# A fused SiLU layer on one core: the first weight slab loaded in two halves, three loads issued from ScalarE, and the first transposed blocks copied by VectorE alone

## Chip, cores and metric

The kernel runs on one core of a Trainium2 chip. The metric is the device time of one execution in microseconds (us), given as the median of several runs of the same program. TensorE is the matrix engine, VectorE and ScalarE the two engines that here copy and evaluate results, GpSimd a fourth one that only prepares constants, and SyncE an engine whose queue issues DMA transfers. ScalarE has a queue that can issue them too. PSUM is the memory that TensorE writes its results to, in eight banks. SBUF is the memory that holds operands.

## What is computed

`x` has 2048 rows of 640, `w1` is 640 x 1728 and `w2` is 1728 x 640, all bf16.

```python
def reference(x, w1, w2):
    h = jnp.einsum("bsd,df->bsf", x, w1)
    h = silu(h)
    out = jnp.einsum("bsf,fd->bsd", h, w2)
    return out
```

## The kernel before

TensorE sums over the partition axis of both its operands, so the first product needs x with its 640 features on partitions. The features are cut into five slabs of 128 (`DT = 5`), the 1728 hidden columns into 13 tiles of 128 (`FT`) and a tail of 64 (`FL`), and the 2048 rows into four chunks of 512 (`SCH`). The result `hT` of the first product keeps the hidden columns on partitions, as the second product needs them.

**Chunks one to three** are brought into `xT` by transposing DMAs (line 153). **Chunk zero** can't wait for those: its four blocks of 128 rows are loaded as they lie, into `x0` (lines 125, 126, 131), and TensorE transposes them, five times 128 x 128 for a block, by a product with an identity matrix. This is the helper `turn` (line 170). The transposed block lies in PSUM and is copied to `xT`: the first three of its five parts by VectorE (line 180) from one bank, the other two by ScalarE (line 188) from a second bank.

**The first weights.** Of w1, the first six tiles of hidden columns (`FA = 6`, 768 columns) are loaded apart from the rest, in five slabs, one for each 128 features (line 129, `ld_k`), 192 KB each. The other columns follow in two larger loads (line 134). All of these transfers, and the loads of x, are issued by SyncE through the helper `load` (line 89), each with a semaphore of its own, in the order x block 0, x block 1, slab 0, slab 1, x block 2, slab 2, x block 3, slab 3, slab 4, the two larger loads. They are issued ahead of a barrier that all engines meet at the start: `barrier_wait_here(ET.SP)` (line 137) moves SyncE's wait for that barrier behind them. ScalarE's wait for it stays at the head of its program. Behind it ScalarE evaluates SiLU once on a small tile (line 147), which brings the function's table in early.

**TensorE's order for chunk zero** is written out by hand in lines 196 to 244. Nine products on a zeroed tile `z` (line 168, `dummies`) run before anything has landed; they write to PSUM bank 3 and nothing reads them. Then the first two blocks are turned, and two more dummies run. The six tiles are accumulated in six PSUM banks at once, slab by slab, by the helper `k_pass(k, j0, j1)` (line 212): for each of the six tiles, one product of slab `k` with the columns of blocks `j0` to `j1`, over the partitions of slab `k`. The hand-written order, with what each step waits for:

```python
wait(pe, *t0, ld_k[0])
k_pass(0, 0, 1, first=True)
wait(pe, *t1)
k_pass(0, 1, 2)
wait(pe, ld_k[1])
k_pass(1, 0, 2)
t2 = turn(2, 7, 6)
wait(pe, ld_k[2])
k_pass(2, 0, 2)
wait(pe, *t2)
```

Then slabs 0 to 2 are used on block 2 alone, block 3 is turned, slab 3 is used on three blocks, slabs 0 to 3 on block 3 alone, and slab 4 on all four. TensorE runs its program in order, so a wait holds everything behind it. In the profile `turn`'s products have line 177, those of every pass have line 204 (the helper `mm`), and the SiLU evaluations have line 208. The seven remaining hidden tiles of chunk zero, the other chunks and the second product follow, and are not touched by the change.

Of the kernel before, what the change touches and what calls it, by code (L numbers as in the profile page):

```python
# [9 lines left out]
def bass_standalone__dense_activation_silu__prompt_kernel(  # L10
# [13 lines left out]
    P = 128  # L24
    NB = 8
    BANK = 512
    DT = D // P
# [10 lines left out]
    pe, act, dve, pool, sp = nc.tensor, nc.scalar, nc.vector, nc.gpsimd, nc.sync  # L38

    with ExitStack() as es:  # L40
        def sb(name, shape, dtype):
            return es.enter_context(nc.sbuf_tensor(name, shape, dtype))
# [3 lines left out]
        w1s = sb("w1s", [P, DT, F], bf16)  # L46
# [14 lines left out]
        def sem(name):  # L61
            s = es.enter_context(nc.semaphore(name))
            count[s.name if hasattr(s, "name") else name] = 0
            return [s, 0]

        def tick(ins, s, n=1):
            ins.then_inc(s[0], n)
            s[1] += n
            return (s, s[1])

        def wait(eng, *points):
            for pt in points:
                if pt is None:
                    continue
                s, v = pt
                key = (id(eng), id(s))
                if seen.get(key, 0) < v:
                    eng.wait_ge(s[0], v)
                    seen[key] = v
# [6 lines left out]
        def load(eng, out_ap, in_ap):  # L86
            s = sem(f"s_ld{n_dma[0]}")
            n_dma[0] += 1
            return tick(eng.dma_start(out=out_ap, in_=in_ap), s, 16)  # L89
# [21 lines left out]
        def barrier_wait_here(engine):  # L111
            lst = nc.main_func.blocks[0].instructions
            lst.append(lst.pop(preamble(engine, "EventSemaphore")))

        x_v = xf.rearrange("(j p) d -> p j d", p=P)
        w1_v = w1.rearrange("(dt p) f -> p dt f", p=P)
        w2_v = w2[0:F0, :].rearrange("(ft p) d -> p ft d", p=P)

        FA = 6
# [4 lines left out]
        p_z = ahead_of_start(lambda: tick(dve.memset(z[:, :], 0.0), s_dve), ET.DVE)  # L124
        ld_x[0] = load(sp, x0[:, 0, :], x_v[:, 0, :])
        ld_x[1] = load(sp, x0[:, 1, :], x_v[:, 1, :])
        ld_k = []
        for k in range(DT):
            ld_k.append(load(sp, w1s[:, k, 0:FA * P], w1_v[:, k, 0:FA * P]))
            if k in (1, 2):  # L130
                ld_x[k + 1] = load(sp, x0[:, k + 1, :], x_v[:, k + 1, :])
        for a, b in FG:
# [33 lines left out]
        def dummies(n):  # L166
            for _ in range(n):
                pe.matmul(ps[:, 3, 0:HB], lhsT=z[:, 0:P], rhs=z[:, :], start=True, stop=True)  # L168

        def turn(j, b_v, b_a):  # L170
            wait(pe, ld_x[j], p_ident, bank_free[b_v], bank_free[b_a])
            v = ps[:, b_v, :].bitcast(bf16)
            a = ps[:, b_a, :].bitcast(bf16)
            nv = DT if b_a == b_v else 3
            for dt in range(DT):
                dst = v[:, dt * P:(dt + 1) * P] if dt < nv else a[:, (dt - nv) * P:(dt - nv + 1) * P]
                ins = pe.transpose(dst, x0[:, j, dt * P:(dt + 1) * P], ident[:, :])  # L177
            t = tick(ins, s_pe)
            wait(dve, t)
            r = tick(dve.tensor_copy(  # L180
                out=xT[:, 0:nv, j * P:(j + 1) * P],
                in_=v[:, 0:nv * P].rearrange("p (k s) -> p k s", s=P),
            ), s_dve)
            bank_free[b_v] = r
            pts = [r]
            if nv < DT:
                wait(act, t)
                r = tick(act.copy(  # L188
                    out=xT[:, nv:DT, j * P:(j + 1) * P],
                    in_=a[:, 0:(DT - nv) * P].rearrange("p (k s) -> p k s", s=P),  # L190
                ), s_act)
                bank_free[b_a] = r
                pts.append(r)
            return pts

        wait(pe, p_z)
        dummies(9)
        barrier_wait_here(ET.PE)
        t0 = turn(0, 7, 6)
        t1 = turn(1, 5, 4)  # L200
        dummies(2)

        def mm(o, l, r, start, stop, shared=False):
            return pe.matmul(o, lhsT=l, rhs=r, start=start, stop=stop, skip_group_check=shared)  # L204

        def silu(out_ap, in_ap, bank, after):
            wait(act, after)
            r = tick(act.activation(out=out_ap, in_=in_ap, func=ACT.Silu), s_act)  # L208
            bank_free[bank] = r
            return r  # L210

        def k_pass(k, j0, j1, first=False, last=False):
            for ft in range(FA):
                if first:
                    wait(pe, bank_free[ft])
                ins = mm(
                    ps[:, ft, j0 * P:j1 * P],
                    w1s[:, k, ft * P:(ft + 1) * P],
                    xT[:, k, j0 * P:j1 * P],
                    start=first, stop=(k == DT - 1), shared=True,  # L220
                )
                if last:
                    silu(hT[:, ft, 0:SCH], ps[:, ft, :], ft, tick(ins, s_pe))

        wait(pe, *t0, ld_k[0])
        k_pass(0, 0, 1, first=True)
        wait(pe, *t1)
        k_pass(0, 1, 2)
        wait(pe, ld_k[1])
        k_pass(1, 0, 2)  # L230
        t2 = turn(2, 7, 6)
        wait(pe, ld_k[2])
        k_pass(2, 0, 2)
# [178 lines left out]
```

## Time and profile before

| | |
|---|---|
| median of 5 runs | 126.49 us (126.29 to 126.83) |
| the profiled execution | 126.29 us |
| its span, first to last instruction | 124.8 us |
| TensorE busy | 122.0 us, 98% of the span |
| ScalarE busy | 39.9 us, 32% |
| VectorE busy | 9.0 us, 7% |
| nine dummies on TensorE | from 0.39 us, 2.10 us |
| first two turns on TensorE | from 2.34 us, 1.25 us |
| two dummies | from 3.38 us, 0.63 us |
| ScalarE's table load (line 147) | from 0.73 us, 1.28 us; its activation from 2.02 us, 0.23 us |
| VectorE's first two copies (line 180) | from 3.10 and 3.63 us, 358 ns each |
| ScalarE's first two copies (line 188) | from 3.09 and 3.63 us, 372 ns each |
| VectorE's wide casts (line 287) | 692 ns for 512 columns, 557 ns for 384, from fp32 |
| one product of 128 columns, of 256 | 219 ns, 272 ns from start to result |
| third and fourth turn, first product | 5.85 and 7.85 us (weights from 5.75 and 7.80 us) |
| first pass of slab 2 | weights from 6.08 us, products from 6.13 us |

Times inside the execution count from the start of its span. A duration is that of one instruction from its start to its result; products are pipelined, so that a row of them takes less than the sum of its durations. The chain of waits goes back from the last instruction: at each step to what released it, or to the instruction before it on its engine. In a window's row the columns are the stretch, its length, the busy time and number of instructions of TensorE, of its weight loads, of VectorE, ScalarE and GpSimd, then the granted clock, the mean busy share of the 16 DMA engines, and the GB/s that they moved. In the row of a DMA issue stand what was moved, the issuing queue (SPq is SyncE's, ACTq ScalarE's), how many, the KB of each, and the median us from issue to landing; a KB here is 1024 bytes.

### The profile page before, as it was taken

The page shows a single profiled execution, that of the slowest core. Times are in us where ns is not written, and L with a number is a line of the kernel's source. Part 1 is how long each engine was busy: PE and PEld are TensorE (multiplying, and loading weights), DVE is VectorE, ACT ScalarE, POOL GpSimd, SP SyncE. Part 2 cuts the span into 40 slices and gives each one's busy share as a digit, 9 for nine tenths or more (in the row PEclk, how much of TensorE's full clock was granted, in tenths as well). Part 3 has the DMA queues.
Part 4 walks back from the last instruction along what each step waited for, and adds up shares of the span by engine and source line. Part 5 has one row for each costly group of instructions (what it writes and reads, how often), then busy time and mean ns, then how long its engine had stood idle before and what let it go on. Part 6 is the DMA issues. An engine that isn't in the chain of part 4 may idle for free.

```text
span 124.8 us, 1496 instructions
## 1 busy us (share of the span) xinstructions
PE 122.0 (98%) x653; PEld 58.4 (47%) x653; DVE 9.0 (7%) x16; ACT 39.9 (32%) x70; POOL 0.8 (1%) x7
## 2 busy tenths in 40 slices
PE   8899999999999999999999999999999999999993
PEld 6686444444444444444444443444444443444452
DVE  0220000000000000000000004202020210112021
ACT  4225955555555555555530003010101001010100
POOL 2000000000000000000000000000000000000000
DMA  6989953446970000000000001341111111111112
GB/s 173 277 265 250 137 115 86 108 102 132 374 271 5 0 0 3 0 0 5 0 0 0 0 0 42 85 147 57 54 53 53 53 53 53 53 58 53 53 59 99
DMA packets 17255, 10.37 MB, mean 83 GB/s; under 512 B 10849, under 2 KB 17249, under 8 KB 17249
## 3 DMA queue, kind: packets, MB, share of 16 engines
q1 hardware_dynamic: 17104, 10.21, 31.2%
q8 instruction: 5, 0.08, 0.3%
q10 hardware_dynamic: 144, 0.07, 0.2%
q14 instruction: 2, 0.01, 0.0%
HBM read 5.16 MB, written 2.62 MB: 62 GB/s over the span
## 4 chain that ended last, share of the span: by engine, by line
PE 95%; DMA 3%; SPq 1%; issue 0%; ACT 0%
PE ps L204 94%; DMA w1s<-in_w_dram 3%; SPq L89 1%; PE ps L177 0%; ACT o_sb L289 0%; SPq L397 0%
## 5 line engine op out<-in xcount | busy, mean ns | idle before, releaser
L204 PE MATMUL ps<-xT,w1s 128*128 128x512 bf16 (+4 forms) x328 | 59.1, 348 | 0.5 <-DMA w1s<-in_w_dram 0.5
L204 PE MATMUL ps<-w2s,hT 128*128 128x512 bf16 (+2 forms) x221 | 45.4, 367 | 0.0
L204 PEld LDWEIGHTS ps<-xT,w1s 128*128 128x128 bf16 (+1 forms) x328 | 28.8, 98 | 30.4 <-DVE xT L180 1.0
L208 ACT ACTIVATE hT<-ps 128x512 bf16<-128x512 f32 x52 | 30.3, 602 | 23.2 <-PE ps L204 23.2
L204 PEld LDWEIGHTS ps<-w2s,hT 128*128 128x128 bf16 x221 | 20.9, 98 | 24.4 <-issue 1.1
L289 ACT CAST o_sb<-ps 128x512 bf16<-128x512 f32 (+1 forms) x8 | 4.4, 545 | 42.2 <-PE ps L204 42.2
L204 PE MATMUL ps<-hT,w2s 128*128 128x512 bf16 x52 | 11.4, 379 | 0.0
L287 DVE CAST o_sb<-ps 128x512 bf16<-128x512 f32 (+1 forms) x9 | 6.1, 677 | 39.9 <-PE ps L204 39.9
L204 PEld LDWEIGHTS ps<-hT,w2s 128*128 128x128 bf16 x52 | 5.0, 97 | 6.3 <-issue 0.4
L287 DVE CAST oT<-ps 128x512 bf16<-128x512 f32 x2 | 1.3, 686 | 66.8 <-PE ps L204 66.8
L289 ACT CAST oT<-ps 128x512 bf16<-128x512 f32 x2 | 1.1, 588 | 11.1 <-PE ps L204 11.1
L168 PE MATMUL ps<-z 128*128 128x256 bf16 x11 | 2.7, 419 | 0.4 <-DVE z L124 0.4
L188 ACT COPY xT<-ps 128x256 bf16<-128x256 bf16 x4 | 1.5, 372 | 5.0 <-PE ps L177 5.0
L204 PE MATMUL ps<-w2t,hTt 64*128 64x512 bf16 (+2 forms) x17 | 2.2, 366 | 0.0
L177 PE MATMUL ps<-ident,x 128*128 128x128 bf16 x20 | 2.1, 265 | 0.0
L180 DVE COPY xT<-ps 128x384 bf16<-128x384 bf16 x4 | 1.4, 358 | 6.9 <-PE ps L177 6.9
L168 PEld LDWEIGHTS ps<-z 128*128 128x128 bf16 x11 | 1.5, 144 | 0.8 <-DVE z L124 0.4
L177 PEld LDWEIGHTS ps<-ident,x 128*128 128x128 bf16 x20 | 1.6, 118 | 0.4 <-DMA x<-in_x_dram 0.3
L208 ACT ACTIVATE hTt<-ps 128x512 bf16<-128x512 f32 x2 | 1.2, 597 | 1.1 <-PE ps L204 1.1
L147 ACT ACT_TABLE_LOAD x1 | 1.3, 1283 | 0.7 <-PEq L397 0.7
L204 PEld LDWEIGHTS ps<-w2t,hTt 64*128 64x128 bf16 x17 | 0.7, 94 | 1.4 <-issue 0.8
L204 PE MATMUL ps<-hTt,w2t 64*128 64x512 bf16 x4 | 0.6, 381 | 0.0
(10 smaller groups left out, 1.5 us busy)
## 6 DMA issues: line engine op xcount, KB each, us to landing
out_dram<-o_sb SPq DMA_DIRECT2D x15, 160.0 KB, 1.8
w2s<-in_w_dram SPq DMA_DIRECT2D x1, 1120.0 KB, 6.6
w1s<-in_w_dram SPq DMA_DIRECT2D x5, 192.0 KB, 3.6
w2s<-in_w_dram SPq DMA_DIRECT2D x1, 960.0 KB, 9.3
x<-in_x_dram SPq DMA_DIRECT2D x4, 160.0 KB, 2.9
w1s<-in_w_dram SPq DMA_DIRECT2D x1, 640.0 KB, 6.7
w1s<-in_w_dram SPq DMA_DIRECT2D x1, 560.0 KB, 7.9
xT<-in_x_dram SPq DMA_TRANSPOSE x15, 2.8
```

Source lines behind the costliest of these rows:

```text
L89: return tick(eng.dma_start(out=out_ap, in_=in_ap), s, 16)
L147: act.activation(out=warm[:, :], in_=warm[:, :], func=ACT.Silu)
L168: pe.matmul(ps[:, 3, 0:HB], lhsT=z[:, 0:P], rhs=z[:, :], start=True, stop=True)
L177: ins = pe.transpose(dst, x0[:, j, dt * P:(dt + 1) * P], ident[:, :])
L180: r = tick(dve.tensor_copy(out=xT[:, 0:nv, j * P:(j + 1) * P], in_=v[:, 0:nv * P].rearrange("p (k s) -> p k s", s=P),), s_dve)
L188: r = tick(act.copy(out=xT[:, nv:DT, j * P:(j + 1) * P], in_=a[:, 0:(DT - nv) * P].rearrange("p (k s) -> p k s", s=P),), s_act)
L204: return pe.matmul(o, lhsT=l, rhs=r, start=start, stop=stop, skip_group_check=shared)
L208: r = tick(act.activation(out=out_ap, in_=in_ap, func=ACT.Silu), s_act)
L287: r = tick(dve.tensor_copy(out=out_ap, in_=in_ap), s_dve)
L289: r = tick(act.copy(out=out_ap, in_=in_ap), s_act)
```

## The change

Slab 0 is loaded in two halves of three tiles each, with a semaphore for each half. The first half is issued by ScalarE, as are slabs 1 and 3; all three stand in ScalarE's program behind its barrier wait and ahead of its SiLU on the small tile. The second half of slab 0, slabs 2 and 4, the blocks of x and the larger loads stay with SyncE, in their order. `turn` takes a new argument: for blocks 0 and 1, VectorE copies all five parts from one bank, and ScalarE none; blocks 2 and 3 are as before. One dummy follows the second turn instead of two. `k_pass` can be limited to some of the six tiles, and slab 0 is used on its first three tiles for block 0, then for block 1, then on the other three for block 0 and block 1, with the wait for the second half between.

```diff
+        FH = 3
+        ld_k0a = load(act, w1s[:, 0, 0:FH * P], w1_v[:, 0, 0:FH * P])
         ld_k = []
         for k in range(DT):
-            ld_k.append(load(sp, w1s[:, k, 0:FA * P], w1_v[:, k, 0:FA * P]))
+            lo = FH if k == 0 else 0
+            q = act if k in (1, 3) else sp
+            ld_k.append(load(q, w1s[:, k, lo * P:FA * P], w1_v[:, k, lo * P:FA * P]))
...
-        def turn(j, b_v, b_a):
+        def turn(j, b_v, b_a, split=True):
...
-            nv = DT if b_a == b_v else 3
+            nv = 3 if split else DT
...
-        t0 = turn(0, 7, 6)
-        t1 = turn(1, 5, 4)
-        dummies(2)
+        t0 = turn(0, 7, 6, False)
+        t1 = turn(1, 5, 4, False)
+        dummies(1)
...
-        def k_pass(k, j0, j1, first=False, last=False):
-            for ft in range(FA):
+        def k_pass(k, j0, j1, first=False, last=False, fts=range(FA)):
+            for ft in fts:
...
-        wait(pe, *t0, ld_k[0])
-        k_pass(0, 0, 1, first=True)
+        wait(pe, *t0, ld_k0a)
+        k_pass(0, 0, 1, first=True, fts=range(FH))
         wait(pe, *t1)
-        k_pass(0, 1, 2)
+        k_pass(0, 1, 2, fts=range(FH))
+        wait(pe, ld_k[0])
+        k_pass(0, 0, 1, first=True, fts=range(FH, FA))
+        k_pass(0, 1, 2, fts=range(FH, FA))
```

## The prediction

> **What bounds the kernel now.** I read the chain of waits first, in order of time (start us, length us, what):
>
> ```profile
> 0.99 3.41 DMA w1s<-in_w_dram
> 4.40 0.14 issue
> 4.53 1.49 PE ps L204 x18
> 6.02 0.28 PE ps L177 x5
> 6.30 1.72 PE ps L204 x24
> 8.02 0.28 PE ps L177 x5
> 8.29 114.60 PE ps L204 x579
> ```
>
> After the first w1 slab lands at 4.40, TensorE never waits again until 122.89. So the change can move the end only by what it does to TensorE's waits in the first 10 us, and one microsecond lost there is lost at the end. Call the slabs k0 to k4 and the blocks of x x0 to x3. The timeline of SyncE's queue gives the times of issue, one every 0.475 us (the nine small loads, then the two large w1 loads):
>
> ```profile
> 0.09 0.86 SPq L89 DMA_DIRECT2D x<-in_x_dram  x2
> 0.99 0.91 SPq L89 DMA_DIRECT2D w1s<-in_w_dram  x2
> 1.94 0.43 SPq L89 DMA_DIRECT2D x<-in_x_dram  x1
> 2.41 0.43 SPq L89 DMA_DIRECT2D w1s<-in_w_dram  x1
> 2.89 0.43 SPq L89 DMA_DIRECT2D x<-in_x_dram  x1
> 3.36 1.95 SPq L89 DMA_DIRECT2D w1s<-in_w_dram  x4
> ```
>
> The issues asked for one at a time from the third on, k0, k1, x2, k2, x3, k3, k4 (last figure: us from issue to landing):
>
> ```profile
> w1s<-in_w_dram SPq DMA_DIRECT2D x1, 192.0 KB, 3.4
> w1s<-in_w_dram SPq DMA_DIRECT2D x1, 192.0 KB, 3.4
> x<-in_x_dram SPq DMA_DIRECT2D x1, 160.0 KB, 3.5
> w1s<-in_w_dram SPq DMA_DIRECT2D x1, 192.0 KB, 3.6
> x<-in_x_dram SPq DMA_DIRECT2D x1, 160.0 KB, 3.8
> w1s<-in_w_dram SPq DMA_DIRECT2D x1, 192.0 KB, 4.1
> w1s<-in_w_dram SPq DMA_DIRECT2D x1, 192.0 KB, 4.9
> ```
>
> Issue plus landing time gives k0 4.40, k1 4.87, x2 5.44, k2 6.01, x3 6.69, k3 7.46, k4 8.73. The delay grows along the queue, from 3.4 to 4.9 us: issuing is not what holds the loads, moving the bytes is. The windows say the same (last two columns: busy share of the DMA engines, GB/s):
>
> ```profile
> 2.00:3.00 1.00, 1.00 (x10) 0.63 (x9) 0.00 (x0) 0.24 (x2) 0.00 (x0) 1.00 0.90 283
> 3.00:4.00 1.00, 1.00 (x8) 0.54 (x6) 0.72 (x2) 0.74 (x2) 0.00 (x0) 1.00 0.96 272
> 4.00:5.00 1.00, 0.49 (x10) 0.50 (x10) 0.00 (x0) 0.00 (x0) 0.00 (x0) 1.00 0.96 261
> 5.00:6.00 1.00, 1.00 (x16) 0.93 (x14) 0.00 (x0) 0.00 (x0) 0.00 (x0) 1.00 0.97 295
> ```
>
> The engines are 90 to 97% busy at a mean of 278 GB/s. The second thing to see is hidden in the chain: between the landing of k0 and the first matmul lie 0.13 us (4.40, 4.53). With the same 0.13, k2, landed at 6.01, allows its pass at 6.14, and that pass does start at about 6.13, when the second turn has ended. k2 is thus on time by nothing. Two limits meet there, and removing the first wait alone exposes the second.
>
> **The change part by part.**
>
> *Order of the loads.* ScalarE's first action behind the barrier is at 0.73 (its table load in the timeline). Three issues at 0.475 us put k0's first half at 0.73, k1 at 1.20, k3 at 1.68. SyncE, with k1 and k3 gone and k0 halved, issues x0 0.09, x1 0.53, k0's second half 0.99, x2 1.47, k2 1.94, x3 2.42, k4 2.89. Merged by time of issue and summed in KB: x0 160, x1 320, first half 416, second half 512, k1 704, x2 864, k3 1056, k2 1248, x3 1408, k4 1600. Before, k2 stood at 1056, x3 at 1216, k3 at 1408. All other places are as they were: k3 has gone ahead of k2 and x3, though it is needed only after both.
>
> *Price of that.* 192 KB are 196.6 thousand bytes, and at 278 GB/s 0.71 us: k2 lands at 6.01 + 0.71 = 6.72. A second price by the landings: place 1248 lies 32/192 of the way from the old place 1216 (6.69) to 1408 (7.46), so 6.82, or 0.81 later. No row shows two queues loading together, so I bound it: 0 if k3's bytes stay behind k2's, 0.81 if all are ahead, and below nothing if two queues together move more than 278 GB/s (the windows from 9 to 11 us show 339 and 355). I take 0.71, since k3 is issued 0.26 us ahead of k2 and the engines have no idle share to carry it in.
>
> The Trainium skill speaks against the change here (DMA: Bandwidth & Descriptors, "Issuing engines are not separate DMA queues"): transfers issued by ScalarE and SyncE run on the same 16 DMA engines and interleave, and a second issuer saves issue time alone. No run shown here has two load queues. By that rule the rate stays and the sum is the one taken; without it the sum would be that of the rival with the higher rate below.
>
> *The split of k0.* The first half stands at 416, halfway from x1's 320 (asked the same way, it landed 2.3 after its issue at 0.53: 2.83) to k0's 512 (4.40): 3.62. Six of the twelve matmuls of 128 columns can then run before 4.53. Their pace is 18 matmuls in 1.49 us, made of 24 column-blocks of 128 and a last result's 0.16 (272 ns less two blocks), so 0.056 each, and six save 0.33. The second half lands where k0 did, 4.40: six matmuls from 4.53 end at 4.87 instead of 5.20. Next late is k1: 4.87 + 0.13 = 5.00 starts its pass, 12 blocks or 0.67 take it to 5.67, the second turn of five transposes (0.28) to 5.95. Then k2 is waited for, and even at its old landing this is until 6.14. So the 0.33 is worth nothing at the end. Shorter rows cost nothing I can see: the large w1 loads, with rows of 1024 and 896 bytes instead of 1536, ran at the 339 and 355 GB/s.
>
> *VectorE alone.* Five blocks instead of three per copy. 384 columns take 358 ns. The fp32 casts of 512 and 384 columns (692, 557 ns) give 1.05 ns a column and 152 ns fixed; with that fixed part bf16 costs 0.54 a column, so 640 columns 496 ns; at 1.05 it would be 627. I take 0.50: the copies run 3.10 to 3.60 and 3.63 to 4.13 (4.38 at the dear end), both under the second half's 4.53. Uncovered, the second would hold six matmuls to 4.2. ScalarE's two copies of 372 ns go.
>
> *Table load and silu's first use* move behind three issues: 0.73 + 1.43 = 2.16, and 1.28 + 0.23 later 3.67. The next work queued there is the third turn's copy, at 6.33 before: covered by 2.7 us.
>
> *One dummy less* takes 0.21 us (2.10 less one result's 0.42, over 8) out of TensorE's wait: nothing on the path, but see the clock.
>
> *SyncE's later issues*, the two large loads and the transposing loads, come 0.95 us earlier but stand behind the same bytes. The first large load lands at 4.31 + 6.7 = 11.0; the first SiLU starts at 10.86, five tiles of 0.22 before the pass ends and that load is needed, some 11.9; the delay adds slack.
>
> *Behind k2*: pass at 6.72 + 0.13 = 6.85 instead of 6.13. x3 lands at k3's old 7.46, needed at 7.80 + 0.72; k3 is early; k4 at 8.73 is needed past 10. Nothing more is lost or won back. **Sum: +0.72 us.** The profiled execution took 126.29 around its span of 124.8, and is the fastest of the five; on it the sum gives 127.01, on the median of 126.49 it gives 127.21. I name the middle, 127.1.
>
> **Rivals.**
>
> *Higher rate, faster.* Two queues fill what one leaves, and the loads run at the 345 GB/s of 9 to 11 us. The bytes through k2, now 1248 KB or 1278 thousand, take 3.70 us from about 1.1, so 4.8, and with x1's lag (328 thousand bytes moved by 2.4, with 222 GB/s from 1 to 2 us and 283 after, landed 2.83) k2 lands near 5.3. Then TensorE is held by the second copy: 4.13 + 0.05, three matmuls (0.17), six (0.33), the k1 pass (0.67), the turn (0.28): k2's pass at 5.63, 0.50 early: 125.99. It decides from about 300 GB/s on, where k2 lands below 6.01. Against it: the engines are already 90% busy and more with one queue. Chance 0.21.
>
> *k3 doesn't get ahead, no change.* If ScalarE's third load starts 0.3 us later than I reckon, or its queue gets the smaller turn, k2 keeps 6.01 and its pass 6.13: 126.49, with 0.3 either way. For it: the margin at issue is only 0.26. Chance 0.17.
>
> *ScalarE late or a cold clock, much slower.* Were the table load issued first, ScalarE's loads would start at 2.01, 2.49, 2.96; k1 would stand behind x3, at 1216 KB, land at 6.69, and its pass start at 6.82 instead of 5.20: 128.1. Against it: the profile gives the table load the line of the activation it serves, L147, which the code has behind the new loads. The clock: nine dummies run at 0.21 per 256 columns, where the passes from 4.53 run at 0.11. The pace doubled between 3.8 and 4.53, after an unbroken busy TensorE since 0.39. If waits and the missing dummy delay that past k2's pass, its 30 blocks (12, then 18) cost 0.05 more each: 1.5, or 128.7. Chance of both 0.10.
>
> The Trainium skill puts that change of pace at some 3.4 us of sustained work (TensorE: Matmul & The Clock Gate, Part 1); by it, the 3.4 us are filled before the first new wait, and the clock costs nothing.
>
> **How the numbers follow.** A measurement of this kernel tells from no change what exceeds 0.3%, 0.38 us: slower is above 126.87, faster below 126.11. The forecast has 0.52, with its own range 126.9 to 127.4 (from the prices 0.71 and 0.81, on 126.29 or 126.49). Slower 0.52 + 0.10 = 0.62, same 0.17, faster 0.21. The range reaches to the faster rival and past the dearer price, 125.9 to 127.6, and leaves out the much slower one.
>
> **What would show it.** Right: in the changed kernel's chain of waits a DMA of w1s ends near 6.7 and TensorE waits some 0.5 to 0.9 us ahead of the third slab's pass; the first matmuls start near 4.2; the rate from 2 to 6 us stays below 300 GB/s; k3 lands before k2. Wrong: TensorE unbroken from about 4.2 on, a rate near 340, k2 landing by 6.0, or ScalarE's issues behind the table load.

## The result and the profile after

The changed kernel takes a median of 126.97 us over 43 runs, the kernel before 126.58 us over 80 runs beside it. The ratio is 1.0028, with a 95% interval from 1.0017 to 1.0038: slower by 0.35 us. The ratio leaves out the few executions that lie more than 1.5% above the fastest of their kernel, so it differs a little from that of the two medians. The forecast's sum was 0.72 us. The direction held and the size came out at half of that sum.

The profiled execution took 126.41 us, the fastest of its 43, so it shows the change at its best. Its chain of waits in order of time (start us, length us, what; the passes now have line 208, the turns line 181 and the dummies line 172, and the lines shift by one or two with other edits):

```profile
0.53 2.95 DMA x<-in_x_dram
3.48 0.05 issue
3.52 0.73 PE ps L181 x5
4.25 0.02 issue
4.28 0.50 DVE xT L184
4.78 0.05 issue
4.83 1.33 PE ps L208 x15
6.16 0.28 PE ps L181 x5
6.43 1.72 PE ps L208 x24
...
8.43 114.60 PE ps L208 x579
```

The wait that sets the end is no longer the first slab's. Block 1 of x lands at 3.48 instead of 2.80. Its turn and VectorE's copy follow, and TensorE runs without a wait from 4.83 on. Slab 2's pass begins at 6.27 instead of 6.13, so this execution loses 0.14 us there.

The timelines of ScalarE and VectorE in the same execution show the moved work:

```profile
0.73 1.34 ACTq L89 DMA_DIRECT2D w1s<-in_w_dram  x3
2.11 1.28 ACT L151 ACT_TABLE_LOAD   x1 [2.11 <-issue]
...
4.28 0.49 DVE L184 COPY xT<-ps 128x640 bf16<-128x640 bf16 x1 [0.71 <-PE ps L181]
```

Three issues from the barrier on, the table load behind them, a copy of five parts in 0.49 us: these stand as the forecast had them. The windows (the last two columns are again the DMA engines' busy share and the GB/s) don't:

```profile
2.00:3.00 1.00, 1.00 (x8) 0.48 (x6) 0.00 (x0) 0.89 (x1) 0.00 (x0) 1.00 0.94 254
3.00:4.00 1.00, 0.51 (x6) 0.48 (x6) 0.49 (x1) 0.62 (x2) 0.00 (x0) 1.00 1.01 329
4.00:5.00 1.00, 0.73 (x10) 0.52 (x8) 0.49 (x1) 0.00 (x0) 0.00 (x0) 1.00 1.02 343
5.00:6.00 1.00, 1.00 (x16) 0.93 (x14) 0.00 (x0) 0.00 (x0) 0.00 (x0) 1.00 1.03 365
```

From 3 to 6 us the loads run at 329 to 365 GB/s, where one queue gave 261 to 295. The forecast kept 278.

Landings, from the trace's semaphore events, in us from the span's start:

| | forecast | this execution | a second one (a_same, below) |
|---|---|---|---|
| block 1 of x | 2.83 | 3.48 | 3.12 |
| slab 0, first half | 3.62 | 3.69 | 3.35 |
| slab 0, second half | 4.40 | 4.37 | 4.91 |
| slab 1 | 4.87 | 4.64 | 5.12 |
| block 2 of x | 5.44 | 5.41 | 5.86 |
| slab 3 | 6.01 (slab 2's old place) | 5.59 | 6.27 |
| slab 2 | 6.72 | 6.01 | 6.45 |

In both, slab 3 lands ahead of slab 2, as forecast. In the first, slab 2 still lands when it did before (5.97 by the same events, where the forecast has 6.01 from a rounded time).

### The profile page after: what moved, and what is told of

Read it like the earlier page. It is cut to its first block, busy times and chain, and to the rows that moved or that the text cites. A ratio compares the mean times of both kernels' runs of the same rounds, so it can differ in the third digit from the quotient of the medians.

```text
span 124.9 us, 1493 instructions
## 1 busy us (share of the span) xinstructions
PE 121.9 (98%) x652; PEld 58.3 (47%) x652; DVE 9.2 (7%) x16; ACT 39.2 (31%) x68; POOL 0.8 (1%) x7
## 4 chain that ended last, share of the span: by engine, by line
PE 95%; DMA 2%; DVE 0%; SPq 0%; issue 0%; ACT 0%
PE ps L208 94%; DMA x<-in_x_dram 2%; PE ps L181 1%; DVE xT L184 0%; SPq L89 0%; ACT o_sb L296 0%; SPq L404 0%
## 5 line engine op out<-in xcount | busy, mean ns | idle before, releaser
L184 DVE COPY xT<-ps 128x640 bf16<-128x640 bf16 (+1 forms) x4 | 1.7, 425 | 6.8 <-PE ps L181 6.8
L192 ACT COPY xT<-ps 128x256 bf16<-128x256 bf16 x2 | 0.7, 372 | 4.5 <-PE ps L181 4.5
```

What stands on the lines that cost most here:

```text
L184: r = tick(dve.tensor_copy(out=xT[:, 0:nv, j * P:(j + 1) * P], in_=v[:, 0:nv * P].rearrange("p (k s) -> p k s", s=P),), s_dve)
L192: r = tick(act.copy(out=xT[:, nv:DT, j * P:(j + 1) * P], in_=a[:, 0:(DT - nv) * P].rearrange("p (k s) -> p k s", s=P),), s_act)
```

## The experiments

Three theories. **K**, the forecast's: slab 3 goes ahead of slab 2, which then lands late. **X**, formed from the profile above: block 1 of x shares the DMA engines with slab 0's first half, lands late, and VectorE's copy holds TensorE. **C**: TensorE is idle for longer, and the pace of its products doubles later. The expectations call this its clock; the granted clock stands at 1.00 in every window, so only the pace of the products shows it. Each kernel was timed in five rounds beside the kernel before; the four of a group ran on one chip.

### First group: undo one part

**a_same** is the changed kernel again.

> The changed kernel once more, for a second profile and a time on the same chip as the next three. Theory K (the forecast's: slab 3 gets ahead of slab 2, which then lands late): ratio to the kernel before 1.003, and slab 2 lands after 6.4 us with TensorE waiting for it. Theory X (the rival formed from the changed kernel's profile: slab 0's first half shares the DMA engines with block 1 of x, which lands some 0.6 us later, and VectorE's longer copy of 0.49 us then holds TensorE): ratio 1.003, block 1 lands after 3.2 us, TensorE starts behind that copy after 4.6 us, and no wait for slab 2.

Measured: 1.0047 (1.0022 to 1.0073). Its chain ends otherwise than that of the first profile:

```profile
1.94 4.51 DMA w1s<-in_w_dram
6.45 0.05 issue
6.49 1.83 PE ps L208 x24
8.33 0.28 PE ps L181 x5
8.61 114.60 PE ps L208 x579
```

Here slab 2, issued at 1.94, lands at 6.45, and its pass starts at 6.49 instead of 6.13: 0.36 us lost, just the median's loss. Block 1 was late as well (3.12), but what it delayed came back in the wait for slab 2. Two executions of one program end on two different waits; one profile could have led to either theory.

**a_k3_sp** gives slab 3 back to SyncE:

```diff
-            q = act if k in (1, 3) else sp
+            q = act if k == 1 else sp
```

> The changed kernel with slab 3 back on SyncE, behind block 3 of x. Theory K: slab 2 gets its old place, the loss of 0.35 us is gone, ratio 1.000. Theory X: block 1 of x still shares with slab 0's first half, so ratio 1.003 as before the edit.

Measured: 1.0012 (0.9994 to 1.0029), 0.35% below a_same on the same chip. K expected 1.000, X 1.003: the interval holds the first and ends just short of the second. Against the 1.0028 of the 43 runs the gain is only 0.16%. Its profile fell on an execution of 127.2 us, which shows something else:

```profile
0.99 4.13 DMA w1s<-in_w_dram
5.12 0.05 issue
5.17 1.77 PE ps L208 x12
6.95 0.28 PE ps L181 x5
7.22 1.72 PE ps L208 x24
```

Slab 1's pass and the rest of slab 0's are 18 column-blocks of 128 and should take about 1.2 us at the pace of the kernel before (18 times 0.056, and 0.16 for the last result); they take 1.77. TensorE's fast pace began only near 6.5 us here. This is taken up again below.

**a_split** copies the first two blocks on both engines again:

```diff
-        t0 = turn(0, 7, 6, False)
-        t1 = turn(1, 5, 4, False)
+        t0 = turn(0, 7, 6)
+        t1 = turn(1, 5, 4)
```

> The changed kernel with the first two blocks copied by VectorE and ScalarE together again. Theory X: the second copy ends 0.13 us earlier, so 0.12 us of the loss come back, ratio 1.002. Theory K: the copies are under the loads, ratio stays 1.003.

Measured: 1.0018 (0.9995 to 1.0041). The interval holds both expectations, so this run is inconclusive. In its profile ScalarE's copy (0.38 us) stands where VectorE's stood, and TensorE starts at 4.85, no sooner than in the changed kernel.

**a_all_sp** puts every load on one queue, the split of slab 0 kept:

```diff
-        ld_k0a = load(act, w1s[:, 0, 0:FH * P], w1_v[:, 0, 0:FH * P])
+        ld_k0a = load(sp, w1s[:, 0, 0:FH * P], w1_v[:, 0, 0:FH * P])
...
-            q = act if k in (1, 3) else sp
+            q = sp
```

> The changed kernel with all loads on SyncE's queue, slab 0 still in two halves, behind block 1 of x. Both theories lose their cause: K because slab 3 is behind slab 2, X because block 1 is ahead of slab 0. Ratio 1.000 by both; block 1 lands at 2.8 us as before. A ratio still near 1.003 would put the cause into the split, the single dummy or VectorE's copies.

Measured: 1.0012 (0.9988 to 1.0036), median 126.99. Block 1 lands at 2.83 again. In the profiled execution (127.47, the slowest of its twelve) TensorE waits 1.2 us for slab 2, issued at 2.89 and landed at 7.30; 15 of its 16 parts had landed by 6.54. The split alone brings nothing. Whether its extra issue, which here delays every later load, costs something, the interval doesn't tell: it holds 1.003, and all twelve runs lie above the median of the kernel before beside them (126.60). So this run does not show that the loss goes with both causes.

### Second group: one part alone, and other orders

**b_k3_first** makes the change of place alone, on the kernel before and its one queue:

```diff
-        for k in range(DT):
+        for k in (0, 1, 3, 2, 4):
...
```

> The kernel before with one change of order on SyncE's queue: slab 3 is issued ahead of slab 2 and block 3 of x. One queue, so nothing shares. Theory K at the forecast's price: slab 2 lands 0.7 us later, at 6.7 us, its pass starts near 6.85, ratio 1.005 to 1.006. Theory X (the loss comes from block 1 of x sharing with slab 0's first half, and VectorE's longer copy): block 1 is untouched, ratio 1.000.

Measured: 1.0054 (1.0033 to 1.0076), which is 0.68 us. The forecast's price for a place in the line was 0.71 to 0.81. X expected nothing. The profiled execution was the slowest of six (127.58); its chain shows the kind of wait:

```profile
2.89 4.52 DMA w1s<-in_w_dram
7.41 0.05 issue
7.46 1.83 PE ps L205 x24
```

Slab 2 is issued at 2.89, one place later than before, and TensorE stands until it lands. Of its 16 parts 15 had landed by 6.79, near the forecast's 6.72; the last came 0.6 us later.

**b_act** moves whole slabs 1 and 3 to ScalarE, without any other part of the change:

```diff
-            ld_k.append(load(sp, w1s[:, k, 0:FA * P], w1_v[:, k, 0:FA * P]))
+            ld_k.append(load(act if k in (1, 3) else sp, w1s[:, k, 0:FA * P], w1_v[:, k, 0:FA * P]))
```

> The kernel before with slabs 1 and 3 issued by ScalarE behind the barrier and nothing else changed: slab 0 whole, two dummies, copies on both engines. Theory K: slab 3 is ahead of slab 2, ratio 1.003 to 1.006. Theory X: slab 1 now takes the place of slab 0's first half beside block 1 of x and delays slab 0 as well; ratio 1.002 to 1.004, with block 1 landing after 3.1 us. Theory R (two queues together move more than one, which is why the forecast's 0.72 us came out at half): 300 GB/s or more from 2 to 6 us, where one queue shows 277.

Measured: 1.0176 (1.0149 to 1.0203), far past what any theory gave, in all six runs (128.21 to 129.34). The chain:

```profile
0.53 4.16 DMA x<-in_x_dram
...
5.87 2.56 PE ps L204 x18
8.43 0.53 PE ps L177 x5
8.97 1.74 PE ps L204 x24
```

Block 1 of x, beside a whole slab on the other queue, lands at 4.69. TensorE's first 18 products then start at 5.87 instead of 4.53 and take 2.56 us instead of 1.49, the turn behind them 0.53 instead of 0.28: the slow pace lasts until near 9 us. Of the 2.7 us that this execution loses, 1.3 come from the late start and 1.3 from the slow pace. Of block 1's 16 parts 15 had landed by 3.10, so what came late is one part, and that sharing caused this is not shown. Why all six runs lie so high was not tried further. The rate from 2 to 6 us was 331 GB/s, as theory R had it.

**v1** keeps one queue, and orders loads and passes by need:

```diff
-            if k in (1, 2):
-                ld_x[k + 1] = load(sp, x0[:, k + 1, :], x_v[:, k + 1, :])
+            if k in (2, 3):
+                ld_x[k] = load(sp, x0[:, k, :], x_v[:, k, :])
...
-        t2 = turn(2, 7, 6)
         wait(pe, ld_k[2])
         k_pass(2, 0, 2)
+        t2 = turn(2, 7, 6)
+        wait(pe, ld_k[3])
+        k_pass(3, 0, 2)
         wait(pe, *t2)
-        for k in range(3):
+        for k in range(4):
             k_pass(k, 2, 3)
         t3 = turn(3, 7, 6)
-        wait(pe, ld_k[3])
-        k_pass(3, 0, 3)
+        wait(pe, ld_k[4])
+        k_pass(4, 0, 3)
         wait(pe, *t3)
         for k in range(4):
             k_pass(k, 3, 4)
-        wait(pe, ld_k[4])
-        k_pass(4, 0, 4, last=True)
+        k_pass(4, 3, 4, last=True)
```

> The kernel before, one queue, but loads and passes in another order: slab 2 ahead of block 2 of x and slab 3 ahead of block 3, and TensorE uses slab 2 on blocks 0 and 1 before it turns block 2, then slab 3, and slab 4 on three blocks before block 3. If the bytes that must have landed at each step set the start (the ground of theory K), each step has about 0.4 us more slack, and a late slab costs less: ratio 0.998 to 1.000. If the waits ahead of slab 1 decide, ratio 1.000.

Measured: 1.0016 (0.9998 to 1.0035), above what either ground expected, though the interval reaches 1.000. In its profile no wait follows slab 0's landing at 4.18:

```profile
4.32 2.54 PE ps L204 x24
```

TensorE's passes begin 0.21 us sooner than in the kernel before. But these 24 products are 36 column-blocks, which take 2.2 us at the pace of the kernel before; the fast pace began only near 5.2 us, and this took back more than the early start gave.

**v2** has this order on the changed kernel, with ScalarE issuing slab 0's first half, slab 1 and block 2 of x.

> The changed kernel with the order of v1; ScalarE issues slab 0's first half, slab 1 and block 2 of x, SyncE all else, so that no load goes ahead of one needed sooner. Theory K: its cause is gone and the second queue's rate is left, ratio 0.997 to 1.000. Theory X: block 1 of x still shares and VectorE still copies alone, ratio 1.001 to 1.003.

Measured: 1.0032 (1.0009 to 1.0054), at the upper end of X's expectation and against K's. Its chain goes through slab 0's second half, landed at 5.31, with block 1 at 3.09. With no slab out of order, the second queue still didn't pay, so K is not all that two queues can lose by.

### Third group: what was priced at nothing, and TensorE's pace

**b_small** is the kernel before with VectorE's copies and the single dummy:

```diff
-            nv = DT if b_a == b_v else 3
+            nv = DT if j < 2 else 3
...
-        dummies(2)
+        dummies(1)
```

> The kernel before with the two edits that the forecast priced at nothing: VectorE alone copies blocks 0 and 1, and one dummy instead of two follows the turns. All loads as before. Theory K (slab 3 ahead of slab 2) and the forecast: the copies end at 4.13 us, ahead of slab 0 at 4.4 us, ratio 1.000. Theory C (waits and the missing dummy leave TensorE idle, and its clock rises later in some executions): the idle time ahead of slab 0 grows by 0.2 us to 0.7 us, ratio 1.001 to 1.002. Theory X (the longer copy holds TensorE): ratio 1.001.

Measured: 0.9999 (0.9980 to 1.0018). In its profile slab 0 happened to land at 4.12, so that the copy was last:

```profile
3.69 0.50 DVE xT L180
4.20 0.05 issue
4.25 1.82 PE ps L204 x18
```

Even uncovered, the copy lets TensorE start at 4.25, earlier than the 4.53 of the kernel before. Its 18 products take 1.82 us instead of 1.49, since the fast pace began near 5.0 here. The times show no cost of the two edits, to about 0.2%.

**a_warm** fills TensorE's idle time in the changed kernel:

```diff
         t0 = turn(0, 7, 6, False)
+        dummies(1)
         t1 = turn(1, 5, 4, False)
-        dummies(1)
+        dummies(3)
```

> The changed kernel with one more dummy between the first two turns and three instead of one behind them, so that TensorE is idle for about 0.6 us less before slab 0's second half. Loads as changed. Theory C: executions with a late clock go, ratio 1.000 to 1.002 instead of 1.003 to 1.005. Theory K: ratio stays 1.003 to 1.005. Theory X: the same, as block 1 and the copy are not moved.

Measured: 1.0007 (0.9986 to 1.0028), as C expected and below the 1.003 of K and X, though its interval meets a_same's. Its profiled execution (127.34) waits for slab 2 all the same:

```profile
1.94 5.23 DMA w1s<-in_w_dram
7.18 0.05 issue
7.22 1.83 PE ps L209 x24
```

Here 15 of slab 2's 16 parts had landed by 6.57.

**a_warm_k3** adds the edit of a_k3_sp to it.

> a_warm with slab 3 back on SyncE behind block 3, as in a_k3_sp (1.0012 there). Theories K and C together: both causes gone, ratio 0.998 to 1.000. Theory X: 1.001 or more is left, since block 1 still shares with slab 0's first half and VectorE copies alone.

Measured: 0.9983 (0.9960 to 1.0005), the lowest of all, not told apart from the kernel before. Taking slab 3 back again gained, 0.24% here and 0.35% in the first group. Their mean is 0.30%; with the half-widths of the four intervals combined as independent (each difference about 0.31, their mean 0.22) it is above nothing. By the same reckoning the added dummies gain as much, 0.40% (a_same to a_warm) and 0.29% (a_k3_sp to a_warm_k3), but these pairs were not timed on one chip. The profile bears on the reason that C gives:

```profile
0.40 2.10 PE ps L172 x9
2.50 0.65 PE ps L181 x5
3.15 0.21 PE ps L172
3.36 0.53 PE ps L181 x5
3.90 0.64 PE ps L172 x3
4.54 2.33 PE ps L209 x18
...
9.15 114.60 PE ps L209 x579
```

TensorE shows no idle time from 0.40 on, starts its passes at 4.54 as the kernel before does at 4.53, and takes 2.33 us for the same 18 products instead of 1.49. The fast pace began near 6.5. Idle time cannot have delayed it in this execution, as the profile shows none. So C's reason is not needed for a late change of pace; that idle time plays no part in the others is not shown, and the times of a_warm leave it open. The late change costs 2.33 - 1.49 = 0.84 us in this execution.

**v3** is v1 with slab 0 in two halves on the one queue, used one after the other as in the changed kernel.

> v1 (one queue, every load in order of need) with slab 0 in two halves, both on SyncE's queue, the first used before the second has landed; the kernel before's copies and two dummies. Theory K: the split lets TensorE start its first six products near 4.0 us, and v1's order leaves no later wait to give it back, 0.2 to 0.3 us less than v1's 1.0016: ratio 0.999 to 1.000. If the split's extra issue (0.475 us on the queue) is what a_all_sp paid for, ratio 1.002 or more.

Measured: 1.0018 (1.0000 to 1.0035), nearer to the 1.002 of the extra issue than to K's 1.000. TensorE's first slab product is at 3.78, yet it later waits for slab 3 until 7.42 (issued at 3.36, landed at 7.37). An early start was given back at a later load, once more. The extra issue delays the later loads only where SyncE issues both halves; in the changed kernel slab 2 is issued at 1.94, where the kernel before has 2.41.

## Why the prediction was right in kind and twice too large

**The bound: right.** A wait in the first 10 us sets the end in the changed kernel's two profiles (in a_k3_sp and a_warm_k3 the late pace does so as well), and nothing that the change saves ahead of slab 2's pass lasts: v3 and the changed kernel both use slab 0 early and end no sooner.

**The order and its price: right on one queue.** Slab 3 goes ahead of slab 2 in every landing table of the change. Done alone on one queue, that costs 0.68 us (b_k3_first), against the 0.71 of the sum. Undone in the changed kernel, it gives back 0.30% with a half-width of 0.22 (against the 43 runs a_k3_sp gains less): some of the 0.28% lost is due to it, and whether all of it is, these runs don't tell.

**The term that was mis-sized: "at 278 GB/s 0.71 us".** The step held the rate of one queue while two were loading, and the price came out smaller: slab 2 landed at its old 6.01 in the first profile and 0.44 us later in the second. From 2 to 6 us the windows give, in GB/s:

| loads on one queue | | loads on two queues | |
|---|---|---|---|
| before | 278 | changed, two profiles | 322, 287 |
| a_all_sp | 233 | a_k3_sp | 286 |
| b_k3_first | 260 | a_split | 325 |
| v1 | 296 | b_act | 331 |
| b_small | 286 | v2 | 296 |
| v3 | 242 | a_warm, a_warm_k3 | 319, 324 |
| mean of 6 | 266 | mean of 8 | 311 |

Two queues move 17% more. From 1 to 6 us the changed kernel's first profile moves 1514 thousand bytes (223 from 1 to 2 us, then the rows above) and the kernel before 1333 (222, then the forecast's rows): 181 more, where slab 3 has 197. So the bytes that went ahead of slab 2 came nearly free in that execution, and slab 2 landed at 6.01 as before. At the second profile's 287 it landed at 6.45, and 0.36 us were lost. The rate alone does not place slab 2, though: at 325 GB/s it landed at 6.24 (a_split), at 319 at 7.18 (a_warm), where its last part came 0.6 us after the others. In the two profiles with slab 3 given back it landed at 6.14 and 5.78. The forecast named the higher rate as its faster rival and set 300 GB/s as the point from which it decides (by its own sum, 1278 thousand bytes from 1.1 us on and a lag of 0.5, some 290 would do). Five of the eight two-queue profiles reached 300, the others lie between 286 and 296, where the one-queue profiles reach too. That fits a loss of half the sum; the share of each execution was not measured. Of the forecast's own signs, the first profile shows those of being wrong (322 GB/s, slab 2 at 6.01) and the second those of being right (287 GB/s, a wait for slab 2).

The Trainium skill's rule (DMA: Bandwidth & Descriptors, "Issuing engines are not separate DMA queues") has a second issuer save issue time alone. Here the table differs from it by 45 GB/s, and the measurement decides. The mean busy share of the engines in these windows rises from 0.92 to 0.98, so their standing still less covers only a part of it.

**A step that failed without deciding the size: "All other places are as they were".** Merging the two queues by time of issue left block 1 of x ahead of slab 0's first half. They share instead: in the seven profiles with a half slab beside it block 1 landed between 3.01 and 3.55, against 2.8 wherever SyncE loads alone. 15 of its 16 parts were there by 2.96 to 3.18, against 2.77 to 2.80, 0.2 to 0.4 us later beside the other load; the rest of the way to 3.48 in the first profile was one late part. There block 1, and not slab 2, is the last wait. X is thus real in the traces; what it adds to the median was not measured apart from K, since a_split was inconclusive.

**Priced at nothing, and nothing:** the copies (0.49 us where 0.50 was reckoned), the dummy, the table load (2.11 to 3.39, where ScalarE's next copy starts at 6.47). b_small gives 0.9999 for the first two.

**The rivals.** The higher rate came in part. "k3 doesn't get ahead" is refuted by the landings. The table load did not go first. A late change of pace occurred, but also in one-queue kernels (b_small, v1) and where TensorE showed no idle time, so the change can't be blamed for it on these runs. Whether it comes more often with two queues is open: there is one profile of each kernel, two of the changed one.

**Luck.** The forecast named 127.1 us, 0.13 from the 126.97 measured. That nearness is luck: the sum was set on 126.29 and on 126.49 and the middle taken, and on the 126.58 that the kernel before took beside it the same sum gives 127.30. The first wait that the sum began from was one execution's, too: slab 0 landed at 4.40 there, with 15 of its 16 parts by 3.54, and at 4.06 to 4.18 in b_k3_first, b_small and v1.

## What to carry to other kernels

Before an early wait is removed, ask what the next one allows: here slab 2 landed just as its pass could start, so an earlier first product was worth nothing. Where the transfers are bound by bytes, a load that is moved to another queue also changes place, and what it overtakes can pay (0.68 us for one place on one queue here); list the landings in the order of need, before and after. One profile of a stage with several near waits shows one of them, so repeat it before naming the cause.

## What had not been expected of the hardware

- A second load queue raised the rate of the same loads on the same 16 engines from a mean of 266 (233 to 296) to 311 GB/s (286 to 331).
- The time at which TensorE's pace doubles varied from 3.8 us (a_same, v3) to 6.5 us (a_k3_sp, a_warm_k3), and came near 9 us in b_act, where TensorE had stood from 3.2 to 4.7. In all of them its work began at 0.4 us. The Trainium skill has it after some 3.4 us of sustained work (TensorE: Matmul & The Clock Gate, Part 1); a_warm_k3 shows 6.1 us of work without a gap ahead of it. About 1.2 us of this work are transposes; whether these count was not tried. Until the change, the passes cost 0.84 us more in that execution, over twice what the change costs.
- One late piece can hold a whole load. Of block 1's 16 parts in b_act, 15 had landed by 3.10 us, and the last came at 4.69. It happens on one queue as well: of slab 0's parts in the kernel before, 15 had landed by 3.54, and the last came at 4.40.
